# Decode attention on one core: K and V cache in 4 MB chunks of 32 KB rows, last V chunk in pieces, wo product before the last PV

## Chip, cores and metric

The kernel runs on one core of one Trainium2 chip. The metric is device time in microseconds (us). It is one program; nothing is exchanged with other cores.

## What is computed

One token is decoded: attention over a long cache, and beside it a dense layer, both of the same normalized input.

```python
B, Sq, D = 1, 1, 512
Hq, Hkv, Sk, Dh = 32, 8, 65536, 128
F = 1792                                   # of the dense layer
q = (xn @ wq).reshape(B, Sq, Hq, Dh)       # xn = layernorm(x)
scores = einsum("bhqd,bhkd->bhqk", q, k) * Dh ** -0.5
p = softmax(scores); o = einsum("bhqk,bhkd->bhqd", p, v)
return x + o.reshape(B, Sq, Hq * Dh) @ wo + gelu(xn @ w1 + b1) @ w2 + b2
```

Everything is bf16. K cache and V cache are 134 MB each, each is read once, and four query heads share one KV head. Weights are wq 4 MB, wo 4 MB, w1 and w2 1.75 MB each.

## The kernel before

**Units.** The 8 KV heads times two halves of 32768 keys make 16 units. A unit has 8 MB of K and 8 MB of V. Of K, every 128x128 tile is transposed on TensorE (function `transposes`, L484) into PSUM tiles `pst` of 8 tiles each, VectorE (L492) and ScalarE (L494) copy these into `kt_ring`, and TensorE multiplies them with the four queries (`scores`, L505). 32 such tiles are a block; `k_block(i)` is the transposes of block i, `scores(u, i)` its product, and `kt_ring` holds 4 blocks. When a unit's 8 blocks are scored, `stats_1` and `stats_2` bring the maximum over partitions (L538, L548, L551) and four exponentials on ScalarE (L557) write the weights `P_bf`. They are used one unit later: `pv` (L573, in `v_block`) multiplies V tiles of the unit before with `P_bf` and adds up in `pO`. So in unit u TensorE works on K of unit u and V of unit u-1.

**Chunks and slots.** K and V come in chunks of `TPD` = 64 tiles, 2 MB: one DMA of 128 rows of 16 KB, one row for a partition. SBUF has 8 slots, four for K and four for V, chunk c of a unit in slot c (or 4 + c). `chunk_order` fixes the order of transfers: K0, K1, V0, K2, V1, K3, V2, V3 in each unit. `issue_chunks` puts the DMAs on SyncE's queue (SP, L407) in exactly this order; an issue waits until TensorE has read the slot's earlier contents (`done_chunk`), and everything behind it on SP waits too. At the start the slots of V hold weights: wq (4 MB in rows of 32 KB, two slots), w1 and w2 (rows of 14 KB). `qproj` (L591), `ffn1` (L606) and `ffn2` (L633) in unit 0 free them. wo comes later in four transfers of 1 KB rows (L427).

**Small loads.** x, b1 and b2 come in four DMAs of ScalarE's queue (L445), in descriptors of 8 and 28 bytes and 1 KB. The first VectorE instruction (L450) waits for all four, and TensorE's first instruction (L457, the moments of the layernorm) waits for VectorE.

**Order on TensorE.** It is written out by hand in `unit`: between the blocks of transposes stand scores and PV of blocks before. Units 1 to 15 are one loop in TensorE's program. After it stand the last unit's statistics, its PV, and the output projection:

```python
stats_1(); stats_2(L); pv(0, 0); pv(0, 1)      # then the softmax sums (L727) and,
pv(1, 0); pv(1, 1)                             # on VectorE, the scaling of all heads -> oT
pv(2, 0); wo_part(oT_bf, "oT", list(range(H))); pv(2, 1); pv(3, 0); pv(3, 1)
```

In the first `wo_part` (L770, 128 matmuls) the last unit's share of its four heads is zero; the second one (16 matmuls) adds it after the last PV has been scaled (L784). A transpose to rows (L788), a cast (L790) and the output DMA (L794) end the program.

Of the kernel before, what the change touches and what calls it, by code (L numbers as in the profile page):

```python
# [224 lines left out]
def bass_parallel_sum__gqa_block_cached__dense_activation_gelu__decode_kernel(  # L225
# [14 lines left out]
    DH = 128  # L240
# [5 lines left out]
    FC = F // 128  # L246
    KT = D // 128
    TPB = 32
    BPC = 2
    TPD = BPC * TPB  # L250
    NC = 4
    NBLK = NC * BPC
    TPU = NC * TPD
    UKEYS = TPU * 128
# [7 lines left out]
    BCOL = TPB * DH  # L262
    assert D % 128 == 0 and F % 128 == 0 and S % UKEYS == 0 and UPG == 2
    assert A_k_cache.shape[3] == DH and H % G == 0 and KT == 4 and HPG == 4
    assert KT * H * DH <= 2 * TPD * DH and KT * F <= TPD * DH and FC * D <= TPD * DH

    SCALE = 1.0 / math.sqrt(DH)
    EPS = 1e-5
# [40 lines left out]
    slot = [kv[:, i * TPD * DH:(i + 1) * TPD * DH].rearrange("p (t d) -> p t d", d=DH)  # L309
            for i in range(NSLOT)]  # L310
    wq_sb = kv[:, NC * TPD * DH:NC * TPD * DH + KT * H * DH].rearrange("p (kt n) -> p kt n", kt=KT)
    w1_at = (NC + 2) * TPD * DH
    w1_sb = kv[:, w1_at:w1_at + KT * F].rearrange("p (kt f) -> p kt f", kt=KT)
    w2_at = (NC + 3) * TPD * DH
    w2_sb = kv[:, w2_at:w2_at + FC * D].rearrange("p (fc n) -> p fc n", fc=FC)
    kt_ring = nc.alloc_sbuf_tensor("kt_ring", [128, NKT * BCOL], BF)
    wo_sb = nc.alloc_sbuf_tensor("wo_sb", [128, H, D], BF)
# [31 lines left out]
    PA_TR = 256  # L349
    PA_SUM = 384  # L350

    csem = [sch.dsem(f"csem{i}") for i in range(NSLOT)]
    sem_misc = sch.dsem("dmisc")
    sem_wq = sch.dsem("dwq")
# [19 lines left out]
    def chunk_order():  # L374
        seq = []
        for u in range(NU + 1):
            ks = [("K", u, c) for c in range(NC)] if u < NU else []
            vs = [("V", u - 1, c) for c in range(NC)] if u > 0 else []
            if ks and vs:
                part = ks[:1]  # L380
                for c in range(1, NC):
                    part += [ks[c], vs[c - 1]]
                part.append(vs[NC - 1])
            else:
                part = ks + vs
            seq.append(part)
        return seq
# [8 lines left out]
    def issue_chunks():  # L396
        while next_chunk[0] < len(chunks):
            kind, u, c = chunks[next_chunk[0]]
            b = slot_of[kind] + c
            if not slot_free[b]:  # L400
                return
            slot_free[b] = False
            g, half = divmod(u, UPG)
            k0 = half * UKEYS + c * TPD * 128
            cache = A_k_cache if kind == "K" else A_v_cache
            src = cache[0, g, k0:k0 + TPD * 128, :].rearrange("(p t) d -> p t d", p=128)
            sch.dma(SP, lambda b=b, src=src: sp.dma_start(out=slot[b], in_=src),  # L407
                    csem[b], writes=[f"slot{b}"])
            next_chunk[0] += 1
            for f in after_chunk.get((kind, u, c), ()):  # L410
                f()

    def dma_wq():
        sch.dma(SP, lambda: sp.dma_start(out=wq_sb, in_=A_wq.rearrange("(p kt) n -> p kt n", kt=KT)),
                sem_wq, writes=[f"slot{NC}", f"slot{NC + 1}"])

    def dma_w12():
        sch.dma(SP, lambda: sp.dma_start(out=w1_sb, in_=B_w1.rearrange("(p kt) f -> p kt f", kt=KT)),
                sem_w12, writes=[f"slot{NC + 2}"], total=32)
        sch.dma(SP, lambda: sp.dma_start(out=w2_sb, in_=B_w2.rearrange("(p fc) n -> p fc n", fc=FC)),  # L420
                sem_w12, writes=[f"slot{NC + 3}"], total=32)

    def dma_wo(q):
        hs = slice(q * H // 4, (q + 1) * H // 4)
# [7 lines left out]
    after_chunk[("K", 0, 0)] = [dma_wq]  # L432
    after_chunk[("K", 0, 1)] = [dma_w12]
    for q in range(4):
        after_chunk[("V", 3 + 2 * q, 1)] = [lambda q=q: dma_wo(q)]
    for b in range(NC, NSLOT):
        slot_free[b] = False

# [92 lines left out]
    def load_q(u):  # L531
        g = u // UPG
        sch.op(DVE, lambda g=g: dve.tensor_copy(out=q_cur[:, :], in_=qT_bf[:, g * HPG:(g + 1) * HPG]),
               reads=["qT"], writes=["q_cur"])
# [28 lines left out]
            )  # L563


    def pv(c, s):
        b = slot_of["V"] + c
        for t in range(TPB):
            tt = s * TPB + t
            gt = c * TPD + tt  # L570
            sch.op(
                PE,
                lambda b=b, tt=tt, gt=gt: pe.matmul(  # L573
                    pO[:, 0:HPG], lhsT=slot[b][:, tt, :], rhs=P_v[:, gt, :],
                    start=gt == 0, stop=gt == TPU - 1),
                reads=[f"slot{b}"] + [f"P_{j}" for j in range(HPG)], writes=["pO"],
                publish=t == TPB - 1,
            )

    def keep_o(u):  # L580
# [5 lines left out]
    def qproj():  # L586
        for h in range(H):
            for kt in range(KT):
                sch.op(
                    PE,  # L590
                    lambda h=h, kt=kt: pe.matmul(  # L591
                        pA[:, PA_Q + h:PA_Q + h + 1], lhsT=wq_sb[:, kt, h * DH:(h + 1) * DH],
                        rhs=xnT_bf[:, kt:kt + 1], start=kt == 0, stop=kt == KT - 1),
                    reads=[f"slot{NC}", f"slot{NC + 1}", "xnT"], writes=["pA"],
                    publish=h == H - 1 and kt == KT - 1,
                )
        sch.op(DVE, lambda: dve.tensor_scalar(out=qT_bf[:, :], in0=pA[:, PA_Q:PA_Q + H], scalar1=SCALE,
                                              scalar2=None, op0=ALU.mult), reads=["pA"], writes=["qT"])
        slot_free[NC] = slot_free[NC + 1] = True

    def ffn1():
        for fc in range(FC):
            for kt in range(KT):
                sch.op(
                    PE,
                    lambda fc=fc, kt=kt: pe.matmul(  # L606
                        pA[:, PA_H + fc:PA_H + fc + 1], lhsT=w1_sb[:, kt, fc:F:FC],
                        rhs=xnT_bf[:, kt:kt + 1], start=kt == 0, stop=kt == KT - 1),
                    reads=[f"slot{NC + 2}", "xnT"], writes=["pA"],
                    publish=fc == FC - 1 and kt == KT - 1,  # L610
                )
        sch.op(DVE, lambda: dve.tensor_tensor(out=h_f[:, :], in0=pA[:, PA_H:PA_H + FC], in1=b1T_bf[:, :],
# [14 lines left out]
    def ffn2():  # L627
        for kt in range(KT):
            cols = slice(kt * 128, (kt + 1) * 128)
            for fc in range(FC):  # L630
                sch.op(
                    PE,
                    lambda kt=kt, fc=fc, cols=cols: pe.matmul(  # L633
                        pA[:, PA_FT + kt:PA_FT + kt + 1], lhsT=w2_sb[:, fc, cols],
                        rhs=gT_bf[:, fc:fc + 1], start=fc == 0, stop=False),
                    reads=[f"slot{NC + 3}", "gT"], writes=["pA"], publish=False,
                )
            sch.op(
                PE,
                lambda kt=kt, cols=cols: pe.matmul(  # L640
                    pA[:, PA_FT + kt:PA_FT + kt + 1], lhsT=rows_bf[:, cols], rhs=ones2_bf[:, :],
                    start=False, stop=True),
                reads=["row0", "row1", "ones2"], writes=["pA"], publish=kt == KT - 1,
            )
        sch.op(DVE, lambda: dve.tensor_copy(out=finT[:, :], in_=pA[:, PA_FT:PA_FT + KT]),
               reads=["pA"], writes=["finT"])
        slot_free[NC + 2] = slot_free[NC + 3] = True

    def done_chunk(kind, c):
        slot_free[slot_of[kind] + c] = True  # L650
        issue_chunks()


    def unit(u, first):
# [8 lines left out]
        if not first:  # L663
            stats_1()
        k_block(1)
        done_chunk("K", 0)
        if not first:
            stats_2(u - 1)
        else:
            qproj()  # L670
            issue_chunks()
        load_q(u)
        k_block(2)
        scores(u, 0)
        k_block(3)
        scores(u, 1)
        done_chunk("K", 1)
        v_block(0)
        v_block(1)
        if first:  # L680
            ffn1()
        else:
            done_chunk("V", 0)
        k_block(4)
        scores(u, 2)
        k_block(5)
        scores(u, 3)
        done_chunk("K", 2)
        v_block(2)
        v_block(3)  # L690
        if first:
            ffn2()
            issue_chunks()
        else:
            done_chunk("V", 1)
        k_block(6)
        scores(u, 4)
        k_block(7)
        scores(u, 5)
        done_chunk("K", 3)  # L700
        v_block(4)
        scores(u, 6)
        v_block(5)
        if not first:
            done_chunk("V", 2)
        scores(u, 7)
        v_block(6)
        v_block(7)
        if not first:
            done_chunk("V", 3)  # L710
            keep_o(u - 1)

    marks = []
# [8 lines left out]
    NE = L * HPG  # L722
    stats_1()
    stats_2(L)
    pv(0, 0)
    pv(0, 1)
    sch.op(PE, lambda: pe.matmul(pA[:, PA_SUM:PA_SUM + NU * HPG], lhsT=ones_f[:, :], rhs=sums[:, :],  # L727
                                 start=True, stop=True),
           reads=["ones_f"] + [f"sums{u}_{j}" for u in range(NU) for j in range(HPG)], writes=["pA"])
# [21 lines left out]
    for h in range(UPG):  # L751
# [5 lines left out]
    sch.op(DVE, lambda: dve.memset(o_c[:, NE:], 0.0), writes=["o_cL"])  # L757
    sch.op(DVE, lambda: dve.tensor_tensor(out=oT_v, in0=oc_v[:, :, 0, :], in1=oc_v[:, :, 1, :], op=ALU.add),
           reads=["o_c", "o_cL"], writes=["oT"])
    done_chunk("V", 0)  # L760
    pv(1, 0)
    pv(1, 1)
    done_chunk("V", 1)

    def wo_part(rhs, res, heads):
        for kt in range(KT):
# [9 lines left out]
        sch.op(DVE, lambda: dve.tensor_tensor(out=finT[:, :], in0=pA[:, PA_AT:PA_AT + KT], in1=finT[:, :],  # L776
                                              op=ALU.add), reads=["pA", "finT"], writes=["finT"])

    pv(2, 0)
    wo_part(oT_bf, "oT", list(range(H)))  # L780
    pv(2, 1)
    pv(3, 0)
    pv(3, 1)
    sch.op(DVE, lambda: dve.tensor_tensor(out=oL_bf[:, :], in0=pO[:, 0:HPG], in1=coef[:, NE:], op=ALU.mult),  # L784
           reads=["pO", "coef"], writes=["oL"])
    wo_part(oL_bf, "oL", list(range(H - HPG, H)))
# [64 lines left out]
```

## Time and profile before

| | before |
|---|---|
| median of 12 runs | 672.84 us (672.75 to 673.02) |
| the profiled execution: its own time / its span | 672.81 us / 671.0 us |
| DMA, mean over the span | 419 GB/s, queue of SP 99.0% of 16 engines |
| TensorE busy (matmul / weight load) | 555.5 us (83%) / 538.9 us (80%) |
| VectorE / ScalarE busy | 288.2 us (43%) / 243.7 us (36%) |
| K and V transfers | 64 and 64 of 2048 KB, 31.6 and 33.8 us from issue to landing |
| transposes L484 | 4096, 332.3 us |
| scores L505 / PV L573 | 4096 each, 122.7 us / 116.7 us |

Times in views count from the start of the span; the 1.8 us by which the execution is longer lie around it. "From issue to landing" includes the time that a transfer stands behind others in the queue. The trace also has a record of every DMA packet with its start, duration and size; here a packet is one row of a transfer.

### The profile page before, as it was taken

How to read it: one execution, taken by the hardware profiler on the slowest of the kernel's cores; microseconds unless marked ns; L12 is line 12 of the kernel's file. 1: busy time of each engine (PE TensorE's matmuls, PEld its weight loads, DVE VectorE, ACT ScalarE, POOL GpSimd, SP SyncE). 2: the span in 40 equal slices, each digit the busy share in tenths (PEclk: the TensorE clock that was granted, in tenths of full speed). 3: DMA queues.
4: the chain of work that ended last, by engine and by line, in shares of the span. 5: the costliest groups of instructions: out<-in, count | busy, mean ns of one | idle time of the engine just before them, and what ended most of it. 6: DMA issues, size and time to landing. Idle time of an engine off the chain costs nothing.

```text
span 671.0 us, 27090 instructions
## 1 busy us (share of the span) xinstructions
PE 555.5 (83%) x12746; PEld 538.9 (80%) x12746; DVE 288.2 (43%) x512; ACT 243.7 (36%) x325; POOL 1.3 (0%) x10
## 2 busy tenths in 40 slices
PE   0899879999988789878898798678977899897876
PEld 0899878989888788878788797678977889796766
DVE  0446434555444334444343544434544445454431
ACT  0234415353533425343252433415343253533330
POOL 0000000000000000000000000000000000000000
PEclk9878867989767977778677787967778678786875
DMA  9999999999999999999999999999999999999994
GB/s 375 419 419 425 421 426 427 428 425 431 419 419 430 425 430 413 426 429 428 429 415 423 430 426 427 416 424 432 427 426 429 427 429 426 426 431 428 425 429 202
DMA packets 23348, 280.82 MB, mean 419 GB/s; under 512 B 2459, under 2 KB 6557, under 8 KB 6557
## 3 DMA queue, kind: packets, MB, share of 16 engines
q1 hardware_dynamic: 23032, 280.50, 99.0%
q8 instruction: 15, 0.25, 0.2%
q10 hardware_dynamic: 292, 0.01, 0.0%
q14 instruction: 9, 0.07, 0.0%
HBM read 280.50 MB, written 0.00 MB: 418 GB/s over the span
## 4 chain that ended last, share of the span: by engine, by line
DMA 58%; PE 34%; ACT 5%; issue 1%; ACTq 0%; DVE 0%
DMA kv<-in_A_k_cache_dram 54%; PE pst L484 23%; PE pO L573 4%; PE pss L505 4%; ACT P_bf L557 3%; DMA rows_bf<-in_B_b_dram 2%; DMA kv<-in_A_v_cache_dram 2%; ACT kt_ring L494 2%; PE pA L538 1%; PE pA L770 1%; PE pA L606 1%; PE pA L591 0%; PE pA L633 0%; ACTq L445 0%; PE pA L788 0%
## 5 line engine op out<-in xcount | busy, mean ns | idle before, releaser
L484 PE MATMUL pst<-ident_bf,kv 128*128 128x128 bf16 x4096 | 332.3, 255 | 81.4 <-DMA kv<-in_A_k_cache_dram 55.3
L484 PEld LDWEIGHTS pst<-ident_bf,kv 128*128 128x128 bf16 x4096 | 306.1, 117 | 92.0 <-issue 34.7
L494 ACT ACTIVATE kt_ring<-pst 128x1024 bf16<-128x1024 bf16 x192 | 194.5, 1021 | 380.1 <-PE pst L484 380.1
L492 DVE COPY kt_ring<-pst 128x1024 bf16<-128x1024 bf16 x320 | 213.3, 689 | 266.4 <-PE pst L484 265.7
L573 PE MATMUL pO<-P_bf,kv 128*128 128x4 bf16 x4096 | 116.7, 165 | 10.1 <-DMA kv<-in_A_v_cache_dram 4.1
L505 PE MATMUL pss<-q_cur,kt_ring 128*128 128x4 bf16 x4096 | 122.7, 165 | 0.8 <-issue 0.8
L573 PEld LDWEIGHTS pO<-P_bf,kv 128*128 128x128 bf16 x4096 | 111.3, 99 | 10.5 <-DMA kv<-in_A_v_cache_dram 4.3
L505 PEld LDWEIGHTS pss<-q_cur,kt_ring 128*128 128x128 bf16 x4096 | 118.4, 98 | 0.9 <-issue 0.9
L557 ACT ACTIVATE P_bf<-scf,negm 128x256 bf16<-128x256 f32 x64 | 49.5, 862 | 7.1 <-DVE negm L551 7.1
L513 DVE COPY scf<-pss 128x512 f32<-128x512 f32 x32 | 22.1, 692 | 63.7 <-PE pss L505 63.7
L517 DVE TENSOR_REDUCE pmax_parts<-scf 128x4 f32<-128x512 f32 x32 | 34.2, 1069 | 1.1
L457 PE MATMUL pA<-st,ones_f 128*128 128x2 f32 x2 | 0.6, 348 | 18.6 <-DVE st L455 18.6
L457 PEld LDWEIGHTS pA<-st,ones_f 128*128 128x128 f32 x2 | 0.5, 310 | 18.6 <-issue 18.6
L557 ACT ACTIVATION_READ_ACCUMULATOR P_bf<-scf,negm 128x1 f32 x64 | 13.7, 214 | 0.0
L538 PE MATMUL pA<-ident_f,pmax 128*4 128x128 f32 x32 | 8.5, 364 | 0.4 <-DVE pmax L525 0.4
L450 DVE CAST xT_f<-xT_bf 128x4 f32<-128x4 bf16 x1 | 0.2, 170 | 17.9 <-DMA rows_bf<-in_B_b_dram 17.9
L548 PEld LDWEIGHTS pA<-diag,ones_f 4*128 4x128 f32 x32 | 4.9, 190 | 2.7 <-DVE diag L542 1.1
L548 PE MATMUL pA<-diag,ones_f 4*128 4x4 f32 x32 | 6.3, 264 | 0.6 <-DVE diag L542 0.6
L468 ACT ACTIVATE mom<-mom 128x1 f32<-128x1 f32 x1 | 0.2, 203 | 16.2 <-DVE mom L466 16.2
L540 DVE TENSOR_REDUCE gmax<-pA 4x1 f32<-4x128 f32 x16 | 4.3, 270 | 0.6 <-PE pA L538 0.6
L606 PE MATMUL pA<-xnT_bf,kv 128*128 128x1 bf16 x56 | 3.6, 197 | 1.0 <-issue 1.0
L606 PEld LDWEIGHTS pA<-xnT_bf,kv 128*128 128x128 bf16 x56 | 3.5, 159 | 1.1 <-issue 1.1
(63 smaller groups left out, 46.9 us busy)
## 6 DMA issues: line engine op xcount, KB each, us to landing
kv<-in_A_k_cache_dram SPq DMA_DIRECT2D x64, 2048.0 KB, 31.6
kv<-in_A_v_cache_dram SPq DMA_DIRECT2D x64, 2048.0 KB, 33.8
kv<-in_A_wq_dram SPq DMA_DIRECT2D x1, 4096.0 KB, 17.0
wo_sb<-in_A_wo_dram SPq DMA_DIRECT2D x4, 1024.0 KB, 38.4
kv<-in_B_w_dram SPq DMA_DIRECT2D x2, 1792.0 KB, 27.7
xT_bf<-in_A_x_dram ACTq DMA_DIRECT2D x1, 1.0 KB
b1T_bf<-in_B_b_dram ACTq DMA_DIRECT2D x1, 3.5 KB
rows_bf<-in_A_x_dram ACTq DMA_DIRECT2D x1, 1.0 KB
```

The lines of the kernel that those rows point to most:

```text
L484: lambda tb=tb, at=at, b=b, tt=s * TPB + t: pe.transpose(pst[tb][:, at * 128:(at + 1) * 128], slot[b][:, tt, :], ident_bf[:, :]),
L492: e, fn = DVE, lambda tb=tb, dst=dst: dve.tensor_copy(out=dst, in_=pst[tb][:, :])
L494: e, fn = ACT, lambda tb=tb, dst=dst: act.activation(out=dst, in_=pst[tb][:, :], func=ACTF.Copy)
L505: lambda sb=sb, col=col, kb=kb, t=t: pe.matmul(pss[sb][:, col * HPG:(col + 1) * HPG], lhsT=kt_ring[:, kb * BCOL + t * 128:kb * BCOL + (t + ...
L513: sch.op(DVE, lambda sb=sb, dst=dst: dve.tensor_copy(out=dst, in_=pss[sb][:, :]), reads=[f"pss{sb}"], writes=[f"scf{k}_{sb}"])
L517: lambda sb=sb, dst=dst: dve.tensor_reduce(out=pmax_parts[:, sb * HPG:(sb + 1) * HPG], in_=dst.rearrange("p (t j) -> p j t", j=HPG), axis= ...
L538: sch.op(PE, lambda: pe.matmul(pA[0:HPG, PA_ST:PA_ST + 128], lhsT=pmax[:, 0:HPG], rhs=ident_f[:, :], start=True, stop=True), reads=["pmax" ...
L548: sch.op(PE, lambda: pe.matmul(pA[:, PA_SB:PA_SB + HPG], lhsT=ones_f[0:HPG, 0:128], rhs=diag4[0:HPG, 0:HPG], start=True, stop=True), reads ...
L557: lambda k=k, u=u, j=j: act.activation(out=P_v[:, :, j], in_=scf_v[k][:, :, j], func=ACTF.Exp, bias=negm[:, u * HPG + j:u * HPG + j + 1], ...
L573: lambda b=b, tt=tt, gt=gt: pe.matmul(pO[:, 0:HPG], lhsT=slot[b][:, tt, :], rhs=P_v[:, gt, :], start=gt == 0, stop=gt == TPU - 1),
L606: lambda fc=fc, kt=kt: pe.matmul(pA[:, PA_H + fc:PA_H + fc + 1], lhsT=w1_sb[:, kt, fc:F:FC], rhs=xnT_bf[:, kt:kt + 1], start=kt == 0, stop ...
L770: lambda kt=kt, k=k, h=h: pe.matmul(pA[:, PA_AT + kt:PA_AT + kt + 1], lhsT=wo_sb[:, h, kt * 128:(kt + 1) * 128], rhs=rhs[:, k:k + 1], star ...
```

## The change

A chunk becomes 4 MB: `BPC` blocks per chunk go from 2 to 4 and `NC` chunks of K (and of V) per unit from 4 to 2, so that a row in SBUF and in the cache is 32 KB and there are 4 slots. wq takes one slot, w1 and w2 share one. The order of transfers in a unit is K0, V0, K1, V1. A K slot is free after four blocks of transposes, where it was two. The order in `unit` is new: blocks 0 to 3 with the PV of V0 behind, then blocks 4 to 7 and the PV of V1; in unit 0 `qproj` stands behind block 2. The last V chunk comes in five DMAs of 64, 32, 16, 8 and 8 tiles (rows of 16, 8, 4, 2 and 2 KB), each with its own semaphore. After the loop the softmax sums stand in front of the whole PV of the last unit's first V chunk, and the first `wo_part` behind it, in front of all of the last chunk's PV.

```diff
-    BPC = 2
+    BPC = 4
-    NC = 4
+    NC = 2
+    LASTP = (64, 32, 16, 8, 8)
+    lsem = [sch.dsem(f"lsem{i}") for i in range(len(LASTP))]
...
             if ks and vs:
-                part = ks[:1]
-                for c in range(1, NC):
-                    part += [ks[c], vs[c - 1]]
-                part.append(vs[NC - 1])
+                part = [x for pair in zip(ks, vs) for x in pair]
...
+            if (kind, u, c) == ("V", NU - 1, NC - 1):
+                t0 = 0
+                for i, n in enumerate(LASTP):
+                    sch.dma(SP, lambda b=b, src=src, t0=t0, n=n: sp.dma_start(
+                        out=slot[b][:, t0:t0 + n, :], in_=src[:, t0:t0 + n, :]),
+                        lsem[i], writes=[f"last{i}"] + ([f"slot{b}"] if i == 0 else []))
+                    t0 += n
...
     # unit(u, first), the new order
+        k_block(0); stats_1(); k_block(1); stats_2(u - 1); load_q(u); k_block(2)
+        # unit 0: no statistics, and qproj(); load_q(u) here, behind k_block(2)
+        scores(u, 0); k_block(3); done_chunk("K", 0)
+        scores(u, 1); v_block(0); scores(u, 2); v_block(1); scores(u, 3); v_block(2); v_block(3)
+        done_chunk("V", 0)
+        k_block(4); k_block(5); k_block(6); scores(u, 4); k_block(7); done_chunk("K", 1)
+        scores(u, 5)                       # unit 0: ffn1() here
+        v_block(4); scores(u, 6); v_block(5); scores(u, 7); v_block(6); v_block(7)
+        done_chunk("V", 1); keep_o(u - 1)  # unit 0: ffn2() in front of done_chunk
...
     stats_1()
     stats_2(L)
-    pv(0, 0)
-    pv(0, 1)
     # softmax sums (matmul), scaling of all heads on VectorE
-    pv(1, 0)
-    pv(1, 1)
-    pv(2, 0)
+    for s in range(BPC):
+        pv(0, s)
     wo_part(oT_bf, "oT", list(range(H)))
-    pv(2, 1)
-    pv(3, 0)
-    pv(3, 1)
+    t0 = 0
+    for i, n in enumerate(LASTP):
+        pv(NC - 1, 0, range(t0, t0 + n), f"last{i}")
+        t0 += n
```

In the part on `unit` the diff is written with several calls on a line. The compute instructions on each engine are as many as before; SP issues fewer DMAs.

More of the change, by code (lines that the diff above doesn't have):

```diff
@@ L264, in bass_parallel_sum__gqa_block_cached__dense_activation_gelu__decode_kernel @@
     assert A_k_cache.shape[3] == DH and H % G == 0 and KT == 4 and HPG == 4
-    assert KT * H * DH <= 2 * TPD * DH and KT * F <= TPD * DH and FC * D <= TPD * DH
+    assert KT * H * DH <= TPD * DH and KT * F + FC * D <= TPD * DH
     SCALE = 1.0 / math.sqrt(DH)
@@ L311, in bass_parallel_sum__gqa_block_cached__dense_activation_gelu__decode_kernel @@
     wq_sb = kv[:, NC * TPD * DH:NC * TPD * DH + KT * H * DH].rearrange("p (kt n) -> p kt n", kt=KT)
-    w1_at = (NC + 2) * TPD * DH
+    w1_at = (NC + 1) * TPD * DH
     w1_sb = kv[:, w1_at:w1_at + KT * F].rearrange("p (kt f) -> p kt f", kt=KT)
-    w2_at = (NC + 3) * TPD * DH
+    w2_at = w1_at + KT * F
     w2_sb = kv[:, w2_at:w2_at + FC * D].rearrange("p (fc n) -> p fc n", fc=FC)
@@ L350, in bass_parallel_sum__gqa_block_cached__dense_activation_gelu__decode_kernel @@
     PA_SUM = 384
+    LASTP = (64, 32, 16, 8, 8)
+    assert sum(LASTP) == TPD
+    lsem = [sch.dsem(f"lsem{i}") for i in range(len(LASTP))]
     csem = [sch.dsem(f"csem{i}") for i in range(NSLOT)]
@@ L406, in issue_chunks @@
             src = cache[0, g, k0:k0 + TPD * 128, :].rearrange("(p t) d -> p t d", p=128)
-            sch.dma(SP, lambda b=b, src=src: sp.dma_start(out=slot[b], in_=src),
-                    csem[b], writes=[f"slot{b}"])
+            if (kind, u, c) == ("V", NU - 1, NC - 1):
[5 more added lines that the diff above has]
+                    t0 += n
+            else:
+                sch.dma(SP, lambda b=b, src=src: sp.dma_start(out=slot[b], in_=src),
+                        csem[b], writes=[f"slot{b}"])
             next_chunk[0] += 1
@@ L414, in dma_wq @@
         sch.dma(SP, lambda: sp.dma_start(out=wq_sb, in_=A_wq.rearrange("(p kt) n -> p kt n", kt=KT)),
-                sem_wq, writes=[f"slot{NC}", f"slot{NC + 1}"])
+                sem_wq, writes=[f"slot{NC}"])
     def dma_w12():
         sch.dma(SP, lambda: sp.dma_start(out=w1_sb, in_=B_w1.rearrange("(p kt) f -> p kt f", kt=KT)),
-                sem_w12, writes=[f"slot{NC + 2}"], total=32)
+                sem_w12, writes=[f"slot{NC + 1}", "w1"], total=32)
         sch.dma(SP, lambda: sp.dma_start(out=w2_sb, in_=B_w2.rearrange("(p fc) n -> p fc n", fc=FC)),
-                sem_w12, writes=[f"slot{NC + 3}"], total=32)
+                sem_w12, writes=["w2"], total=32)
     def dma_wo(q):
@@ L434, in bass_parallel_sum__gqa_block_cached__dense_activation_gelu__decode_kernel @@
     for q in range(4):
-        after_chunk[("V", 3 + 2 * q, 1)] = [lambda q=q: dma_wo(q)]
+        after_chunk[("V", 3 + 2 * q, 0)] = [lambda q=q: dma_wo(q)]
     for b in range(NC, NSLOT):
@@ L563, in stats_2, with pv @@
             )
-    def pv(c, s):
+    def pv(c, s, ts=range(TPB), res=None):
         b = slot_of["V"] + c
-        for t in range(TPB):
+        for t in ts:
             tt = s * TPB + t
@@ L575, in pv @@
                     start=gt == 0, stop=gt == TPU - 1),
-                reads=[f"slot{b}"] + [f"P_{j}" for j in range(HPG)], writes=["pO"],
-                publish=t == TPB - 1,
+                reads=[res or f"slot{b}"] + [f"P_{j}" for j in range(HPG)], writes=["pO"],
+                publish=t == ts[-1],
             )
@@ L593, in qproj @@
                         rhs=xnT_bf[:, kt:kt + 1], start=kt == 0, stop=kt == KT - 1),
-                    reads=[f"slot{NC}", f"slot{NC + 1}", "xnT"], writes=["pA"],
+                    reads=[f"slot{NC}", "xnT"], writes=["pA"],
                     publish=h == H - 1 and kt == KT - 1,
@@ L598, in qproj @@
                                               scalar2=None, op0=ALU.mult), reads=["pA"], writes=["qT"])
-        slot_free[NC] = slot_free[NC + 1] = True
+        slot_free[NC] = True
     def ffn1():
@@ L608, in ffn1 @@
                         rhs=xnT_bf[:, kt:kt + 1], start=kt == 0, stop=kt == KT - 1),
-                    reads=[f"slot{NC + 2}", "xnT"], writes=["pA"],
+                    reads=[f"slot{NC + 1}", "w1", "xnT"], writes=["pA"],
                     publish=fc == FC - 1 and kt == KT - 1,
@@ L635, in ffn2 @@
                         rhs=gT_bf[:, fc:fc + 1], start=fc == 0, stop=False),
-                    reads=[f"slot{NC + 3}", "gT"], writes=["pA"], publish=False,
+                    reads=[f"slot{NC + 1}", "w2", "gT"], writes=["pA"], publish=False,
                 )
@@ L646, in ffn2 @@
                reads=["pA"], writes=["finT"])
-        slot_free[NC + 2] = slot_free[NC + 3] = True
+        slot_free[NC + 1] = True
     def done_chunk(kind, c):
@@ L665, in unit @@
         k_block(1)
-        done_chunk("K", 0)
         if not first:
             stats_2(u - 1)
-        else:
+        load_q(u) if not first else None
+        k_block(2)
+        if first:
             qproj()
-            issue_chunks()
-        load_q(u)
-        k_block(2)
+            load_q(u)
         scores(u, 0)
         k_block(3)
+        done_chunk("K", 0)
         scores(u, 1)
+        v_block(0)
+        scores(u, 2)
+        v_block(1)
+        scores(u, 3)
+        v_block(2)
+        v_block(3)
+        if not first:
+            done_chunk("V", 0)
+        k_block(4)
+        k_block(5)
+        k_block(6)
+        scores(u, 4)
+        k_block(7)
         done_chunk("K", 1)
-        v_block(0)
-        v_block(1)
+        scores(u, 5)
         if first:
             ffn1()
[L682 to L690, printed above, removed]
+        v_block(4)
+        scores(u, 6)
+        v_block(5)
+        scores(u, 7)
+        v_block(6)
+        v_block(7)
         if first:
@@ L695, in unit @@
             done_chunk("V", 1)
[L696 to L710, printed above, removed]
             keep_o(u - 1)
@@ L759, in bass_parallel_sum__gqa_block_cached__dense_activation_gelu__decode_kernel @@
            reads=["o_c", "o_cL"], writes=["oT"])
-    done_chunk("V", 0)
-    pv(1, 0)
-    pv(1, 1)
-    done_chunk("V", 1)
+    for s in range(BPC):
+        pv(0, s)
     def wo_part(rhs, res, heads):
```

## The prediction

> **What bounds the kernel now.** The page comes first.
>
> ```profile
> span 671.0 us, 27090 instructions
> ...
> DMA  9999999999999999999999999999999999999994
> GB/s 375 419 419 425 421 426 427 428 425 431 419 419 430 425 430 413 426 429 428 429 415 423 430 426 427 416 424 432 427 426 429 427 429 426 426 431 428 425 429 202
> ...
> q1 hardware_dynamic: 23032, 280.50, 99.0%
> ```
>
> The 16 DMA engines are full from the first slice to the last; TensorE at 83% has gaps. So the length is 280.5 MB through a queue that never runs dry, plus what lies before the first byte and behind the last. The queue's own waits say why it never does:
>
> ```profile
> SPq L407 <- PE pst L484: 371.5, 48, 29.7
> SPq L407 <- PE pO L573: 150.5, 51, 18.9
> ```
>
> SP waits for slots nearly all the time, and yet a K chunk lands 31.6 us after its issue: some six transfers always stand in front of it. Slots come free long before their refill is due. Two places are different. At the start (timeline):
>
> ```profile
> 17.91 0.17 DVE L450 CAST xT_f<-xT_bf 128x4 f32<-128x4 bf16 x1 [17.91 <-DMA rows_bf<-in_B_b_dram]
> ...
> 19.03 6.53 PE L484 MATMUL pst<-ident_bf,kv 128*128 128x128 bf16 x64
> ...
> 25.41 3.36 PE L591 MATMUL pA<-xnT_bf,kv 128*128 128x1 bf16 x128
> ```
>
> TensorE idles until the small loads land, though K0 landed at 8 us. At the end (timeline):
>
> ```profile
> 635.99 3.53 PE L484 MATMUL pst<-ident_bf,kv 128*128 128x128 bf16 x32 [1.64 <-DMA kv<-in_A_k_cache_dram]
> ...
> 648.18 0.59 PE L538 MATMUL pA<-ident_f,pmax 128*4 128x128 f32 x2 [0.39 <-DVE pmax L525]
> ...
> 653.39 1.87 PE L573 MATMUL pO<-P_bf,kv 128*128 128x4 bf16 x64 [3.41 <-ACT P_bf L557]
> ...
> 660.42 1.01 PE L573 MATMUL pO<-P_bf,kv 128*128 128x4 bf16 x32 [2.94 <-DMA kv<-in_A_v_cache_dram]
> 661.29 3.55 PE L770 MATMUL pA<-oT_bf,wo_sb 128*128 128x1 bf16 x128
> 664.71 2.70 PE L573 MATMUL pO<-P_bf,kv 128*128 128x4 bf16 x96
> ...
> 669.44 0.35 SPq L794 DMA_DIRECT2D out_dram<-fin_bf  x1
> ```
>
> The last K chunk lands at 635.9. TensorE needs 12.2 us to L538, 5.2 us of statistics and exponentials, then waits for V until 660.4, and works 10.6 us from there to the end (the last V packet ends at 664.9 by the packet records). So up to 635.9 DMA sets the time; behind it DMA and TensorE are close.
>
> **1. Wider rows.** The packet records of the trace price a row. Before 30 us the starts of neighbouring packets on an engine lie 607 ns apart for 16 KB and 1209.5 ns for the 32 KB rows of wq: the same bytes in one row save 4.5 ns. Later 16 KB costs more: transfers 100 to 130 land 147.09 us apart, 4.903 us each, which is 8 packets of 612.1 ns and a semaphore write of 6 ns. Open is whether these 5.1 ns follow rows or bytes. Most neighbours lie 610.5 ns apart, and every fourth descriptor, the semaphore's counted, has 7 ns more: that speaks for rows. With rows, a 4 MB transfer saves 8 x (2 x 612.1 - 1214.6) + 6 = 83 ns; with bytes, 8 x 4.5 + 6 = 42 ns; if the late cost went altogether, 8 x (1224.2 - 1209.5) + 6 = 124 ns. I take rows. The last K chunk has 61 such transfers up to its landing: **-5.1 us** (2.6 to 7.6). [...] The 128 rows of wq, at the 32 KB pitch that K and V get, all took 1213 ns, which is full rate.
>
> **2. Start.** K0 doubles to 4 MB in front of wq. The last of the small loads' descriptors is passed at 17.6, just after wq's last packet: each waits for one large packet. Eight packets of K0 are now 602 ns longer, so L450 moves from 17.9 to 22.7 and the transposes from 19.0 to 23.9. That alone costs nothing, since weights and K keep the queue busy: before, w2 was through at 31.0 on most engines; two chunks with 2 MB more each make that 40.6. By then the next K0 must be issued, and its slot is free only after block 3: 96 transposes (64 took 6.5, the rest at 1.9 per 32: 8.4), `qproj` 3.4, 0.6 for VectorE's two q copies, now uncovered, scores 0.8, transposes 1.9 to 3.6: 39.0 to 40.7, the middle 39.9. From issue to first packet it was 1.3 us at the start, so 41.2 (40.3 to 42.0) against 40.6: **+0.6** for an idle queue (0 to 1.4). The transposes take 3.5 us per 32 while the granted clock is halved and 1.9 at full clock; here the clock records have full speed from 25.0 on, 6.0 us after the first transpose. The Trainium skill ("TensorE: Matmul & The Clock Gate", Part 1) says the window is 3.4 us and free-running; by an estimate from that, between 3.4 and 6.8 us, which would put the issue 1.2 us earlier to 0.4 us later than the row does.
>
> **3. Later refills.** Units 1 and 2 are TensorE's own in the profile before: unit 1 lasts 40.3 us (58.6 to 98.9; some 5 us of it waits for instructions), unit 2 lasts 36. A unit of transfers takes 38.9. Before, unit 1 began 23.7 us behind block 3 (34.9 to 58.6); the same work from 39.9 on makes it begin at 63.6 and unit 2 at 103.9. The next K0 is issued when block 3 is through, 13.5 us into a unit (58.6 to 71.9, 98.9 to 112.5): at 77.1 and 117.4. Due it is when the queue has served four transfers more, less the 1.3 us of its own start: 41.2 + 38.9 - 1.3 = 78.8, then 117.7. It just fits. From then on TensorE gains some 3 us a unit. SP issues in order, but V0, K1 and V1 behind come free in just that order, with 4 to 6 us to spare. **+0.3** (0 to 2.5). The new order on TensorE costs nothing while DMA covers it; a unit is 13.7 us to the end of block 3, 5.9 of scores and PV, 15.4 for the rest, 35.0 in all.
>
> **4. Last unit.** Blocks 0 to 3 and V0 of unit 15 take 19.6 us, as long as the two transfers from K0's landing to K1's, so K1 may wait: **+0.3** (0 to 1.5). From K1's landing two more blocks than before are open: 12.2 + 3.7 to L538, 5.2 to the last exponential, 0.4 for the sums (L727), 3.5 for 128 PV, 3.4 for wo, 3.5 for 128 PV, 3.6 from the last PV to the end (667.4 to 671.0): 35.5 us, against 671.0 - 635.9 = 35.1: **+0.4** (-1 to +2). The last piece lands 29.5 us after K1 (two transfers of 9.7 and pieces of 10.1, by 537 ns for 14 KB and 48 for 1 KB), and 0.2 of PV and 3.6 behind it would end at 33.3. So TensorE ends last, the pieces gain nothing by themselves, and their longer DMA time is hidden by these 2.2 us. Moving wo ahead moves work on an engine that has no gap left there; before, 2.9 us of gap stood at 660. The pieces' issue waits on SP for V1 of unit 14 (read 15.4 after K1's landing); due it is at 18. The added waits on TensorE are five, one ahead of each piece's PV; behind them stands only the end of the program, and by this sum none of them waits.
>
> **Sum**: 672.81 (the profiled execution; the median is 672.84) - 5.1 + 0.6 + 0.3 + 0.3 + 0.4 = 669.3 us. About 0.2% (1.35 us) can be told from no change.
>
> **Rivals.**
> A, the forecast: 669.3, by itself 667.4 to 671.2; chance 0.50.
> B, the late cost follows bytes: -2.6 in place of -5.1, 671.8. For it: 610.5 against 607 is not tied to every fourth descriptor. Chance 0.17.
> C, slower: the queue runs dry at the start. Mechanism: a 4 MB K slot returns after four blocks, and TensorE starts 4.8 us late. Price: each microsecond by which a K0 refill misses its due time (39.3, 78.8 and 117.7 by parts 2 and 3) is lost for good. It decides from a miss of 4.4 us (5.1 less the 0.7 of part 4); instruction waits as in unit 1 (5 us), met in unit 0 on top of the 0.9 of parts 2 and 3, would give a miss of about 6: 672.8 - 5.1 + 6 + 0.7 = 674.4. For it: the margins are 1.7 and 0.3 us. Against it: the instruction waits of unit 1 are in the sum already, and unit 2 had none. Chance 0.14.
> D, the late cost goes: fewer transfers stand queued, as in the first 30 us, when packets were short; -7.6, no idle queue, part 4 as above: 665.9. Chance 0.12.
> E, the end pays: TensorE reaches the pieces with nothing left over, the end is 33.3 us behind K1, 2.2 less than in A: 667.1. Against it: the sum of rows in 4. Chance 0.07.
>
> Faster by over 0.2% (below 671.5): nearly all of A, D, E and a third of B, 0.72. Within 0.2%: most of B, a bit of A and C, 0.15. Slower: most of C and a bit of B, 0.13. The range 666.0 to 672.8 leaves out half of D and most of C.
>
> **What would show it.** Right: 32 KB packets at 1213 to 1217 ns; slices near 430 GB/s with no gap but at most one near 41 us; L450 at 22.7; K's last landing at 631 to 633; TensorE without a wait from there to the end except for the exponentials, and PV of the pieces not waiting for DMA. Wrong: packets of 1220 ns or more (B); DMA share below 9 in a slice near 40, 78 or 117 us (C); PV waiting for V's pieces (E).

## The result, and the profile after

The changed kernel takes 679.25 us (median of 7 runs, 678.24 to 680.74) against 672.87 us for the kernel before in the same comparison: a ratio of 1.0096 (95% interval 1.0086 to 1.0105). A second comparison gave 1.0094 (1.0077 to 1.0111). It is about 1% slower; the forecast was 669.3 us. The profiled run took 678.35 us, its span is 676.6 us, 5.6 more than before.

The page of the changed kernel, first the lines that answer to those of before:

```profile
span 676.6 us, 26982 instructions
...
DMA  9959999999999999999999999999999999999993
GB/s 372 426 228 431 431 427 426 417 434 430 422 426 434 425 432 418 432 430 434 432 419 430 428 432 429 420 434 430 428 434 426 434 428 429 434 432 434 430 402 161
...
q1 hardware_dynamic: 14392, 280.50, 97.3%
```

The same 280.5 MB go through in 14392 packets in place of 23032. 20 of the 40 slices stand at 430 GB/s or above, where 6 did before. The third slice (34 to 51 us) stands out: 228 GB/s, the one hole in an otherwise full row. Here are 2 us pieces of it (columns: the stretch and its length, busy time of PE, PEld, DVE, ACT and POOL with their instructions, granted clock, DMA share, GB/s):

```profile
38.00:40.00 2.00, 1.86 (x75) 1.76 (x71) 0.00 (x0) 0.00 (x0) 0.00 (x0) 1.00 1.03 431
40.00:42.00 2.00, 0.21 (x3) 0.16 (x3) 0.00 (x0) 0.00 (x0) 0.00 (x0) 0.74 0.15 57
42.00:44.00 2.00, 1.51 (x41) 1.48 (x40) 0.36 (x2) 0.00 (x0) 0.00 (x0) 0.50 0.04 8
44.00:46.00 2.00, 2.00 (x21) 2.00 (x20) 0.69 (x1) 1.02 (x1) 0.00 (x0) 0.50 0.00 0
46.00:48.00 2.00, 2.00 (x56) 2.00 (x53) 0.69 (x1) 0.99 (x1) 0.00 (x0) 0.56 0.12 33
48.00:50.00 2.00, 2.00 (x71) 2.00 (x68) 0.55 (x1) 0.04 (x1) 0.00 (x0) 1.00 1.02 311
```

For some 8 us the DMA engines have nothing to move. By the packet records w2 lands at 40.7 and the next K0 18.0 us later, where two 4 MB transfers that follow each other without a gap land 9.7 apart: 8.3 us are lost. The timeline shows why the K0 refill was issued so late:

```profile
27.51 0.17 DVE L458 CAST xT_f<-xT_bf 128x4 f32<-128x4 bf16 x1 [27.51 <-DMA rows_bf<-in_B_b_dram]
...
28.64 8.12 PE L492 MATMUL pst<-ident_bf,kv 128*128 128x128 bf16 x96
...
36.59 3.27 PE L599 MATMUL pA<-xnT_bf,kv 128*128 128x1 bf16 x125
...
41.79 0.24 PE L599 MATMUL pA<-xnT_bf,kv 128*128 128x1 bf16 x3 [1.94 <-issue]
...
43.40 3.57 PE L492 MATMUL pst<-ident_bf,kv 128*128 128x128 bf16 x32
...
47.01 0.33 SPq L415 DMA_DIRECT2D kv<-in_A_k_cache_dram  x1
```

VectorE's first instruction (L458, L450 before) gets the small loads at 27.5 us, not at 17.9. The whole chain to the end of block 3 hangs on it, and in `qproj` TensorE waits another 1.94 us for "issue": the profile knows no semaphore that it waits for. SP issues at 47.0, 6 us after the queue ran dry. The end (timeline; L768 is `wo_part`, L581 is PV):

```profile
639.16 6.71 PE L492 MATMUL pst<-ident_bf,kv 128*128 128x128 bf16 x96
...
654.56 0.58 PE L546 MATMUL pA<-ident_f,pmax 128*4 128x128 f32 x2 [0.38 <-DVE pmax L533]
...
660.32 3.60 PE L581 MATMUL pO<-P_bf,kv 128*128 128x4 bf16 x128
663.78 2.11 PE L768 MATMUL pA<-oT_bf,wo_sb 128*128 128x1 bf16 x74
667.54 1.60 PE L768 MATMUL pA<-oT_bf,wo_sb 128*128 128x1 bf16 x54 [1.65 <-issue]
669.01 3.61 PE L581 MATMUL pO<-P_bf,kv 128*128 128x4 bf16 x128
```

K1, the last K chunk, lands at 639.0 (packet records). From there it takes 37.6 us to the end of the span, where it took 35.0 to 35.1 from the last K chunk before. No PV of a piece waits for DMA, but `wo_part` has an "issue" wait of 1.65 us.

So the 5.6 us are: the last K chunk lands 3.0 us later (639.0 against 636.0, which is 8.3 of hole less 5.3 of faster transfers), and the end behind it is 2.6 longer. Each of these three parts is tried below.

### The profile page after: what moved, and what is told of

Its sections match the earlier page's. It is cut to its first block, busy times and chain, and to the rows that moved or that the text cites. A ratio compares the mean times of both kernels' runs of the same rounds, so it can differ in the third digit from the quotient of the medians.

```text
span 676.6 us, 26982 instructions
## 1 busy us (share of the span) xinstructions
PE 545.8 (81%) x12746; PEld 530.0 (78%) x12746; DVE 287.6 (43%) x512; ACT 242.0 (36%) x325; POOL 1.3 (0%) x10
## 3 DMA queue, kind: packets, MB, share of 16 engines
q1 hardware_dynamic: 14392, 280.50, 97.3%
## 4 chain that ended last, share of the span: by engine, by line
DMA 47%; PE 38%; ACT 11%; issue 2%; DVE 1%; ACTq 0%
DMA kv<-in_A_k_cache_dram 43%; PE pst L492 25%; ACT P_bf L565 7%; PE pO L581 5%; PE pss L513 4%; ACT kt_ring L502 4%; DMA rows_bf<-in_B_b_dram 4%; PE pA L546 1%; PE pA L768 1%; PE pA L614 1%; PE pA L599 0%; DVE pmax_parts L525 0%; PE pA L641 0%; ACTq L453 0%; DVE scf L521 0%
## 5 line engine op out<-in xcount | busy, mean ns | idle before, releaser
L492 PE MATMUL pst<-ident_bf,kv 128*128 128x128 bf16 x4096 | 316.8, 251 | 81.5 <-DMA kv<-in_A_k_cache_dram 57.5
L492 PEld LDWEIGHTS pst<-ident_bf,kv 128*128 128x128 bf16 x4096 | 297.2, 115 | 91.1 <-DMA kv<-in_A_k_cache_dram 59.0
L581 PE MATMUL pO<-P_bf,kv 128*128 128x4 bf16 x4096 | 119.9, 165 | 8.0 <-issue 8.0
L581 PEld LDWEIGHTS pO<-P_bf,kv 128*128 128x128 bf16 x4096 | 113.6, 100 | 8.3 <-issue 8.3
L513 PEld LDWEIGHTS pss<-q_cur,kt_ring 128*128 128x128 bf16 x4096 | 116.0, 98 | 0.6 <-DVE q_cur L541 0.6
L458 DVE CAST xT_f<-xT_bf 128x4 f32<-128x4 bf16 x1 | 0.2, 170 | 27.5 <-DMA rows_bf<-in_B_b_dram 27.5
L768 PE MATMUL pA<-oT_bf,wo_sb 128*128 128x1 bf16 x128 | 3.7, 165 | 1.7 <-issue 1.7
```

The costliest lines, as they stand in the source:

```text
L492: lambda tb=tb, at=at, b=b, tt=s * TPB + t: pe.transpose(pst[tb][:, at * 128:(at + 1) * 128], slot[b][:, tt, :], ident_bf[:, :]),
L513: lambda sb=sb, col=col, kb=kb, t=t: pe.matmul(pss[sb][:, col * HPG:(col + 1) * HPG], lhsT=kt_ring[:, kb * BCOL + t * 128:kb * BCOL + (t + ...
L581: lambda b=b, tt=tt, gt=gt: pe.matmul(pO[:, 0:HPG], lhsT=slot[b][:, tt, :], rhs=P_v[:, gt, :], start=gt == 0, stop=gt == TPU - 1),
L768: lambda kt=kt, k=k, h=h: pe.matmul(pA[:, PA_AT + kt:PA_AT + kt + 1], lhsT=wo_sb[:, h, kt * 128:(kt + 1) * 128], rhs=rhs[:, k:k + 1], star ...
```

## The experiments: the start

Theory 1, formed on reading the two traces: the small loads are what is late. The packet records show them on ScalarE's queue (q10) beside the large ones of SP (q1): an engine passes one small descriptor, then one whole large packet, then the next small one. Their spacing is 613 ns while 16 KB rows pass and 1215 ns while 32 KB rows pass. An engine has some 20 of them.

**x on a semaphore of its own.** VectorE and TensorE need only x at first; in the changed kernel they wait for all four small loads.

```diff
+    sem_x = sch.dsem("dx")
-        sch.dma(ACT, ..., sem_misc, writes=[res], total=64)
+        sch.dma(ACT, ..., sem_x if res == "xT_bf" else sem_misc,
+                writes=[res], total=16 if res == "xT_bf" else 48)
```

> The changed kernel, with x's small load on a semaphore of its own, so that VectorE's first instruction waits for x alone and not for b1 and b2. Theory 1 (idle queue): the small loads stand behind one 32 KB packet per descriptor, TensorE starts at 28.6 instead of 19.0, the first refill of a K slot comes 7.8 us late. Then L458 moves from 27.5 to about 13, the DMA row shows no slice below 9 near 41 us, the last K1 lands near 631 and the time falls by 7.8, to 670.5 to 671.5 us. Theory 2 (grain alone): a 4 MB slot comes back too late whatever the start, so part of the hole stays and the time stays above 676. Theory 3 (TensorE late for the whole program): the time falls by as much as TensorE starts earlier, about 14 us, to 665.

Measured: 671.42 us (670.62 to 672.1), ratio to before 0.9977 (0.9967 to 0.9986). Timeline and page of this run:

```profile
8.61 0.17 DVE L460 CAST xT_f<-xT_bf 128x4 f32<-128x4 bf16 x1 [8.61 <-DMA xT_bf<-in_A_x_dram]
```

```profile
GB/s 374 421 438 421 430 429 431 428 430 436 413 434 432 429 430 420 430 430 430 434 413 434 432 431 423 424 430 430 434 430 432 428 432 433 432 430 429 432 379 127
```

The third slice is full (438 GB/s), and 7.8 us of the median are gone with one semaphore; x came at 8.61, earlier than the 13 that was expected. Without the wait for all four small loads there is no hole.

**The same on the kernel before.**

> The kernel before with the same edit. Theory 1: its queue was never idle, so an earlier start of TensorE is worth nothing, although L450 moves from 17.9 to about 6: 672.5 to 673.1 us. Theory 3: TensorE's start carries through to the end, some 10 us less, 663.

Measured: 672.88 us, ratio 0.9999 (0.9989 to 1.0008), although VectorE starts at 5.91 in place of 17.91. Here, where the queue never ran dry, an earlier start of TensorE is worth nothing. The edit is no gain of its own; it takes away what the change had added.

**Rows of 16 KB in the new order.** Each 4 MB chunk as two DMAs of half rows, everything else as in the changed kernel.

```diff
-                sch.dma(SP, ... sp.dma_start(out=slot[b], in_=src), csem[b], ...)
+                hh = TPD // 2
+                sch.dma(SP, ... sp.dma_start(out=slot[b][:, 0:hh, :], in_=src[:, 0:hh, :]), csem[b], ...)
+                sch.dma(SP, ... sp.dma_start(out=slot[b][:, hh:, :], in_=src[:, hh:, :]),
+                        csem2[b], writes=[f"half{b}"])
     # transposes and PV wait for both halves
```

> The changed kernel with each 4 MB chunk in two DMAs of 16 KB rows on semaphores of their own; TensorE still waits for both before it reads a chunk, and slots, order and tail stay as changed. Theory 1: the small loads wait for packets half as long while K0 is loaded, L458 is near 19, no idle queue, but a chunk takes 9.81 us again instead of 9.72: last K1 at 635.9 as in the kernel before, then the changed kernel's end of 37.9 us: 674 to 676 us. Theory 2 (grain alone): the hole of 7.8 us stays and the rows' gain is lost: 684. If rows did not matter for the rate: 671.

Measured: 675.51 us (674.82 to 676.8), ratio 1.0045 (1.0028 to 1.0062). The small loads come at 12.86, earlier than expected:

```profile
12.86 0.17 DVE L462 CAST xT_f<-xT_bf 128x4 f32<-128x4 bf16 x1 [12.86 <-DMA rows_bf<-in_B_b_dram]
```

The queue has no hole, the halves land 4.905 us apart as before, and K1 lands at 635.6. So the order of transfers and the 4 MB slots are not what makes the start late; the length of the rows is, since it sets how long a small descriptor waits. (The slots do set how much slack a late start leaves: a slot comes back behind four blocks.) And this run prices the rows: with 32 KB rows and no hole K1 lands at 630.6 to 630.7 (x alone, K0 held), 5.0 us earlier. The loss of 2.6 us against before is all at the end (37.4 us behind K1).

**Is it the same in every run?** In the first profile of the changed kernel all small descriptors came behind the first 32 KB packet of each engine (the first of them starts at 3.64 us, the 16 first large ones at 1.76 to 2.74); in the other kernels' profiles some of them passed ahead of the first one. So the unchanged version of the changed kernel ran again, and beside it one in which SP's first issue waits for the first memset on POOL, a delay of 0.22 us.

```diff
-        sch.op(POOL, lambda t=t: pool.memset(t[:, :], 0.0), writes=[res])
+        ev_ms = sch.op(POOL, lambda t=t: pool.memset(t[:, :], 0.0), writes=[res], publish=True)
+        if res == "ident_bf":
+            sch.wait_ev(SP, ev_ms)
```

> The changed kernel once more. Question: are its small loads late in every run, or only in the run that was profiled? In that run the first small descriptor came behind two 32 KB packets on every engine, in all other kernels the first four or five came ahead of the first large one. Theory 1 (the order at the start is a race that this program loses nearly every time, because its first issue on SP comes a few ns earlier beside ScalarE's): L458 again at 26 to 28, queue idle 6 to 8 us near 41, 678 to 680 us. Theory 2 (the one profile was a bad draw): L458 near 22 to 23, idle queue 1 to 3 us, and single times down to 673 to 675.

> The changed kernel with SP's first issue (K0) held until the first memset on POOL is through, about 0.25 us; nothing else differs. Theory 1 (who comes first at the start decides some 4 us of the small loads' delay): the first four to ten small descriptors of each engine pass before the first 32 KB packet, L458 comes at 21 to 23 in place of 27.5, the queue is idle for 1 to 3 us near 41, time 672.5 to 675.5. Theory 2 (the order at the start is worth nothing; the small loads trail whatever comes first): L458 at 27 to 28, 679 to 680.

Measured, the changed kernel again: 678.8 us; its profiled run was the fastest of four (676.24; the others 678.63 to 679.94), and there the loads came at 22.98 us:

```profile
22.98 0.17 DVE L458 CAST xT_f<-xT_bf 128x4 f32<-128x4 bf16 x1 [22.98 <-DMA rows_bf<-in_B_b_dram]
...
37.24 0.24 PE L599 MATMUL pA<-xnT_bf,kv 128*128 128x1 bf16 x3 [1.70 <-issue]
...
38.85 3.57 PE L492 MATMUL pst<-ident_bf,kv 128*128 128x128 bf16 x32
...
42.46 0.33 SPq L415 DMA_DIRECT2D kv<-in_A_k_cache_dram  x1
```

Here the first small descriptor came 0.2 us before the first large packet. So the landing is a draw (22.98 and 27.51 were seen). Both theories expected one thing of all runs, and neither was wholly right. This draw has the small loads where the forecast put them (22.7), and it still loses 3.3 to 3.6 us of queue at the first refill. K1 lands at 635.0, 0.9 earlier than before the change; that this run is still slower than before comes from its end, 39.4 us.

Measured, K0 held: 671.73 us (670.48 to 672.94), ratio 0.9983 (0.9973 to 0.9992), 7 us better than the changed kernel from holding its first transfer back by 0.22 us. It beat the 672.5 to 675.5 that was expected of theory 1. Timeline of this run:

```profile
0.96 0.40 SPq L417 DMA_DIRECT2D kv<-in_A_k_cache_dram  x1
...
19.29 0.17 DVE L460 CAST xT_f<-xT_bf 128x4 f32<-128x4 bf16 x1 [19.29 <-DMA rows_bf<-in_B_b_dram]
...
33.28 0.24 PE L601 MATMUL pA<-xnT_bf,kv 128*128 128x1 bf16 x3 [1.42 <-issue]
...
38.49 0.33 SPq L417 DMA_DIRECT2D kv<-in_A_k_cache_dram  x1
```

All of x's descriptors passed before the first 32 KB packet, those of b1 and the two rows behind it at one for each large packet. The refill is issued at 38.5, 2 us before the queue would run dry, and no hole opens: the transfers land 9.8 to 10.0 us apart at first and 9.72 later.

## The experiments: the end

These stand on the version with x on its own semaphore, in which the start is out of the way (671.42).

**One piece.** `LASTP = (128,)` in place of five.

> As x_alone, with the last V chunk in one DMA of 32 KB rows instead of five pieces. Theory 1 with the sum of the end (TensorE is still at work on wo when the last piece lands): within 0.5 us of x_alone. Rival (the pieces let PV start early): 3 us slower than x_alone, the price of 128 PV.

Measured: 671.05 us (670.48 to 672.13), ratio 0.9974 (0.9963 to 0.9986). The falling pieces are worth nothing here.

**wo behind the first piece's PV.**

```diff
-    wo_part(oT_bf, "oT", list(range(H)))
     t0 = 0
     for i, n in enumerate(LASTP):
         pv(NC - 1, 0, range(t0, t0 + n), f"last{i}")
+        if i == 0:
+            wo_part(oT_bf, "oT", list(range(H)))
```

> x_alone with the wo product of all heads behind the first piece's PV (64 tiles) instead of in front of all of the last chunk's PV. Theory (behind K1's landing TensorE has no gap, so the order of its work is free): within 0.5 us of x_alone, 671.0 to 671.9. Rival (wo in front is what hides it behind V's landing): 2 to 3 us slower, 673.5 to 674.5.

Measured: 671.2 us (670.84 to 672.07), the same. Here, where no PV behind K1's landing waits for DMA, the order of TensorE's work is free.

**wo in a gap that is left.** TensorE idles while ScalarE computes the last exponentials. The heads of the first seven KV heads need nothing of the last two units: their sums, scaling and 112 of the 128 wo matmuls move into this gap, 16 stay behind the PV of the first chunk.

```diff
-    stats_1()
-    stats_2(L)
-    # sums, scaling of all heads; PV of the first chunk; wo of all heads
+    ce, pse = heads_a("E", 0, GE)              # GE = 7: sums (into a free PSUM tile)
+    stats_1()
+    heads_b("E", 0, GE, ce, pse)
+    stats_2(L)
+    heads_c("E", 0, GE, HE * UPG)              # scaling
+    wo_part(oT_bf, "oTE", list(range(HE)))     # 112 matmuls
+    # sums of the last KV head, PV of the first chunk, scaling
+    wo_part(oT_bf, "oTL", list(range(HE, H)), HE)
```

> x_alone with the heads of KV groups 0 to 6 scaled and multiplied with wo as soon as the loop is over, in the 4 to 5 us in which TensorE waits for the last unit's statistics and exponentials; the last group's four heads (16 matmuls) behind the PV of the last unit's first V chunk. Theory (TensorE's work behind K1's landing sets the end): 112 of 128 matmuls, 3 us and what code fetch they carry, move into a gap, and the time falls by 3 to 5 us, to 666.4 to 668.4. Rival (the last V bytes set the end): within 0.5 us of x_alone.

Measured: 668.75 us (668.59 to 668.89), ratio 0.9938 (0.9921 to 0.9954), 2.7 less than with x alone. Timeline:

```profile
649.97 3.15 PE L780 MATMUL pA<-oT_bf,wo_sb 128*128 128x1 bf16 x112 [1.41 <-DVE oT_bf L771]
...
653.41 2.49 PE L583 MATMUL pO<-P_bf,kv 128*128 128x4 bf16 x88
657.75 1.20 PE L583 MATMUL pO<-P_bf,kv 128*128 128x4 bf16 x40 [1.86 <-issue]
```

The wo product lies in the gap, but the "issue" wait did not go with it: it stands in the PV now, 1.86 us, and keeps the gain under the 3 to 5 hoped for. It is 0.6% faster than the kernel before, where x alone and K0 held are 0.2% faster.

**The tail of the change on the kernel before.** Pieces of 32, 16, 8 and 8 tiles, and wo ahead of the last two PV parts, with the 2 MB chunks otherwise kept.

> The kernel before (2 MB chunks, 16 KB rows, its own order) with the change's two edits of the end alone: the last V chunk in pieces of 32, 16, 8 and 8 tiles, and the wo product in front of the last two V chunks' PV. There TensorE had a gap of 3.0 us at 657.4. Theory: wo fills it, PV of the last tiles starts as they land, and the end is the last landing near 664.9 + 0.25 + 3.6: 2.2 us earlier, 670.2 to 671.2. Rival (waits for code, as in the changed kernel's wo, take the gain): 672 to 673.

Measured: 672.2 us (671.93 to 672.39), ratio 0.999 (0.998 to 0.9999), a gain of 0.7 where 1.7 to 2.7 had been expected. Timeline:

```profile
660.38 1.68 PE L780 MATMUL pA<-oT_bf,wo_sb 128*128 128x1 bf16 x57 [1.04 <-issue]
661.93 2.03 PE L583 MATMUL pO<-P_bf,kv 128*128 128x4 bf16 x71
664.95 1.68 PE L583 MATMUL pO<-P_bf,kv 128*128 128x4 bf16 x57 [0.99 <-issue]
```

The DMA wait of 2.9 us in the kernel before is gone, and two "issue" waits of 1.04 and 0.99 stand in its place. The time lies in the rival's range.

**The last V chunk in a K slot.** With wo in the gap, the last chunk goes to slot 0 of K, which is free earlier; then the same with one piece.

```diff
-            b = slot_of[kind] + c
+            b = 0 if (kind, u, c) == ("V", NU - 1, NC - 1) else slot_of[kind] + c
```

> x_alone_early_wo with the last V chunk in the first K slot, which is free long before, in place of the slot that TensorE empties 16 us behind K1's landing. In x_alone_early_wo the queue is idle for 2.6 us on its earliest engines in front of the pieces. Theory (TensorE's work behind K1's landing, waits for code included, sets the end): the last V packet ends 2 to 3 us earlier, near 657.5 to 658.5, and the time stays within 0.5 us, 668.2 to 669.2. Rival (the pieces' landing sets the end): 2 us faster, 666.5.

> early_wo_kslot with the last V chunk in one transfer. Theory: TensorE reaches this chunk near 659.2, the single transfer lands on its slowest engine near 659.5, so pieces are worth at most 0.5 us: 668.3 to 669.4. Rival (the pieces pay once wo is out of the way): 3 us slower than early_wo_kslot.

Measured: 668.52 us (668.2 to 669.02), ratio 0.9937 (0.992 to 0.9953), and 669.11 us (668.77 to 669.62) with one piece. The time is the same to 0.2 us, but the last piece lands only 0.5 us earlier (660.1 for 660.6), not the 2 to 3 that were expected, so the two times alone do not tell the theories apart. The timelines do: in both versions no PV of a piece waits for DMA, so TensorE's work sets the end. Five pieces against one are worth 0.6 us here at most. 668.5 is the best time found, 0.6% under the kernel before.

## Why the prediction was wrong

**The rows (part 1) were right.** Forecast: 9.723 us for a 4 MB transfer, -5.1 us at the last K chunk. Measured: 16 transfers of the changed kernel land 155.55 us apart, 9.722 each, the packets take 1216 ns, and K1 lands 5.0 us earlier than with half rows. The saving follows rows, not bytes; B and D fall.

**The start (part 2) is the step that failed.** It put the K0 refill's issue at 39.9 and the loss at 0.6 us; it was issued at 47.0, and the loss was 8.3. Of the 7.1 us:
- 4.8 are the small loads: 27.5 for 22.7. "Eight packets of K0 are now 602 ns longer" counted the packets of before. It took the trace's order at the start, where some small descriptors had passed ahead of the first large packet, as given; it is a draw, and here all of them came behind, one for each 32 KB packet.
- 2.0 are `qproj`: 5.4 us for 3.4, by an instruction wait of 1.9. The prediction had read such waits in unit 1 and put them in a rival. The profile before had them in unit 0 as well, in `ffn1` (timeline before: `38.37 1.78 PE L606 MATMUL pA<-xnT_bf,kv 128*128 128x1 bf16 x28 [1.04 <-issue]`), and the sum had no term for them there.
- 0.8 are block 3's transposes: 3.57 us at a granted clock of 0.50, the upper of the two rows that the text gave, where the middle was taken. The first 96 took 0.4 to 0.5 less than the sum had.

The second profile of the changed kernel separates these: with the landing near the forecast (22.98) the issue came at 42.46, 2.6 late, by the two other terms, and 3.3 to 3.6 us were lost. So the sum had two faults, and either was enough for a hole (the late loads alone make 39.9 into 44.7). The mechanism was written down, as rival C, with the right place. Its chance of 0.14 was too small. It named margins of 1.7 and 0.3 us, those of the second and third refill; at the first there was none (39.9 against a due time of 39.3), and three of the terms there were read from rows that had other conditions.

"The Trainium skill" says in "DMA: Bandwidth & Descriptors", Queues, rings and completion order, that an engine goes round its queue rows in turn and drains a whole packet of one, typically 9 to 17 descriptors, before it switches. The packet records agree with the turn and not with the size: one row of 16 or 32 KB lies between two small descriptors (613 and 1215 ns).

**Later refills (part 3) were right in size.** No second hole opens. Behind the first refill the transfers land 9.8 to 9.9 us apart for some 70 us, as they also do with x alone, and then 9.72. One comes 0.3 to 0.4 us late, K0 of unit 3 (10.08 behind the transfer before it, 10.15 in the second profile), against 0.3 forecast.

**The end (part 4) was under-counted:** 0.7 forecast (0.3 and 0.4), 2.6 measured. In other profiles with the same end it is 2.4 (16 KB rows), 3.7 (K0 held), 4.4 (the changed kernel again) and 4.5 (x alone). From K1's landing to the first PV it took 21.3 us for 21.5. From there it took 16.3 for 14.0: wo 5.2 for 3.4, with 1.65 us of "issue", and 7.6 for 7.1 from the last chunk's PV on, of which 0.3 is the output's DMA. That TensorE would end last and the pieces gain nothing was right. "An engine that has no gap left there" was the wrong half of it: the gap of 2.9 us before had covered a wait that came into the open when the gap was closed. In those other profiles the same wait is 1.6 to 2.2. Most of the rest of the spread goes with the clock: the 96 transposes behind K1's landing take 6.71 us in the changed kernel, where the granted clock returns from 0.5 to full 2.5 us after their start, 6.92 after 3.0 (K0 held), 7.81 after 4.8 (x alone) and 8.26 after 5.8 (the changed kernel again).

What these "issue" waits are is argued, not shown. In each profile a 16 KB packet of an instruction queue (q8) lies beside the wait: in the changed kernel from 39.3 to 40.4 for the wait from 39.9 to 41.8, and from 665.2 to 666.3 for that from 665.9 to 667.5. The first such wait of each end, and that of `qproj`, ends 1.2 to 1.5 us after its packet. "The Trainium skill" ("Runtime: NRT & Kernel Launch", Instruction fetch mechanics) says that the fetch of sequential code is mostly hidden. If these waits are fetches, it is not hidden here: 1.0 to 2.5 us stand open in the straight code behind the loop.

**The sum made again** with the measured terms: for K0 held, 672.8 - 5.3 (K1's landing, 630.7 against 636.0) + 3.7 (the end, 38.7 against 35.0) = 671.2, which is its profiled run's time. The changed kernel has 8.3 more from the hole and 1.1 less at the end: 678.4 for 678.35. So even the faultless start would have missed 669.3 by 2 us, on account of part 4.

Open stays why the clock returns later in some runs, and why the start's draw falls as it does: two profiles of the changed kernel show two orders, both with SP's first issue at 0.74, and only the held K0 shows what 0.22 us on SP are worth.

## What to carry to other kernels

A small load that the first compute waits for is paid for by the row length of whatever is queued beside it, one row for each of its descriptors; before rows are widened, give the needed load a semaphore of its own or send it ahead of the first big one. Doubling the chunk halves the slots. A refill whose forecast issue lies within 1 us of its due time, by a sum of rows from other conditions, has no margin: take the upper row of every term when the loss is one-sided. A gap that a trace shows on an engine may cover a second wait; what closing it brings is the gap less what stands behind.

## What the runs showed of the hardware

- A small descriptor on another queue costs one large packet: 613 ns beside 16 KB rows, 1215 ns beside 32 KB.
- Holding SP's first issue back by 0.22 us let all of x's descriptors pass ahead of the first large packets and took 7 us off the changed kernel. Without the hold the order differed between two profiles of the same kernel.
- A 32 KB row is passed in 1216 ns where two of 16 KB take 1224, also at the power-of-two pitch of 32 KB.
- Straight TensorE code stood 1.0 to 2.5 us in "issue" near the end of the program; the wait moved to another instruction when the order was changed.
- The same 96 transposes took 6.71 to 8.26 us, the longer the later the granted clock returned from 0.5 to full (2.5 to 5.8 us after their start).
